# Value products of both halves joined in one group, folds moved to VectorE, first weights behind the last norm

## The chip, the cores and the metric

The kernel runs on one core of one Trainium2 chip. The metric is the device time of one execution, in microseconds (us). The engines are TensorE (PE, matrix products into PSUM), VectorE (DVE), ScalarE (ACT), GpSimd (POOL) and SyncE (SP, which issues transfers). They run side by side, each works off its own queue in order, and they wait for one another through semaphores.

## What is computed

The reference has two parts. The first is chunked attention over 4 batches, 8 heads, 768 positions and 64 columns; each chunk of 32 positions sees its own keys, 16 to the left, 8 to the right and 8 memory keys:

```python
for c in range(nc):
    k_full = np.concatenate([mem_k, k_ctx], axis=2)
    v_full = np.concatenate([mem_v, v_ctx], axis=2)
    scores = scale * np.matmul(q_c, k_full.transpose(0, 1, 3, 2))
    a = np.exp(scores - max); a = a / sum(a)
    out[:, :, c_start:c_end] = np.matmul(a, v_full)
```

The second takes the result as x (4 batches of 768 x 512) through a Fourier mix, a norm and a two-layer network:

```python
X = np.fft.fft(np.fft.fft(x, axis=1), axis=2)
u = x + np.real(X)
un = (u - mean(u)) / np.sqrt(var(u) + 1e-06)
out = u + np.maximum(un @ w_ch1, 0.0) @ w_ch2      # 512 -> 2048 -> 512
```

## The kernel before

**A planner writes the order.** The kernel does not issue its instructions directly. It adds tasks to a `Plan` (lines 37 to 174): an engine, an estimated cost, a function that emits the instructions, the tasks that must be done before, and buffers that are taken and given back (`take`, `give`; with `pick`, whichever of several comes free first). A small event loop then places the tasks, engine by engine, and the instructions are emitted in that order. A task that isn't ready is passed over for a later one of the same engine, so that `ph` and `pc`, which have low rank, fill the holes of attention and Fourier. `behind=` holds a task back until another is placed; `lag=` asks that its inputs have been done for so long already; neither puts a wait into the program. On the chip each engine follows that order strictly.

**Attention** (`attention(n)`, line 869) runs over 16 pairs of heads, four for each batch (HP = 4). For each pair q and k are loaded by POOL's queue (line 347) and v by SP's (line 350), q and k are turned on PE (`trq`, `trk`, line 374) and copied out (`qT`, `kTb`); in batch 3 a transposing transfer does that. Then, for each half g of the positions: scores on PE into `sc` (line 430, 12 matmuls, tile 64*128), two exponentials on ACT (line 438) into one of three `e1` buffers, the value products on PE into `xa` (line 454, 12 fp32 products that the profile shows as 24 matmuls, tile 128*64), and the norm on DVE (lines 464 and 465) into `xsb`. `xa` is one PSUM bank. In batch 0 the second half goes to a bank of `mlp`, named `xo`.

**PSUM** has further banks: `tr` for the turned q and k, `sc`, and two each of `mlp` and `acc`, which `ph`, `pc`, `ps`, `pm`, `tp` share.

**The first Fourier stage** (`first_fourier`, line 983) belongs to batch 0. It folds x in pieces while the pairs of batch 0 finish: `g_zy` (line 594) after two pairs, `g_ff` (lines 608 to 615) once after the third and once after the fourth, then the split into high (ACT, line 629) and low parts (DVE, line 633), and the row transform on PE (`ps`, lines 653 and 666). Until they can begin, PE runs `idle` matmuls (line 830). The first two folds of the half g = 1 are on POOL (`early = ("DVE", "POOL")[g]`); all others are on DVE. Then come `up` (ACT, 538), its rest (DVE, 543), the column transform (`pm`, 677), the sum and the statistics (DVE, 683 and 691), `un` (ACT, 697), and in batch 0 its turn on PE (`tp`, 704) and the copy `unT` (715). The later batches use `fourier(b)` with whole folds on DVE.

**The network** runs over all batches: for each half of the rows 16 blocks `ph` (line 739, four matmuls of 384 columns, then a relu on ACT, line 747), then `pc` (line 754, 16 matmuls of 512 columns for each of three row tiles) and the output sum on DVE (line 779). Its weights w1 and w2 are loaded by POOL's queue (`weights`, lines 975 and 979): w1 behind the k load of pair 5, w2 behind that of pair 6.

Of the kernel before, what the change touches and what calls it, by code (L numbers as in the profile page):

```python
# [177 lines left out]
def kernel(  # L178
# [15 lines left out]
    P = 128  # L194
# [25 lines left out]
    def bank(tag, shape, dtype, name):  # L220
        i = bank_free[tag].pop(0)
        t = fps.tile(shape, dtype, tag=f"{tag}{i}", bufs=1, name=name)
        bank_of[name].append((t, tag, i)) if name in bank_of else bank_of.update({name: [(t, tag, i)]})
        return t
# [125 lines left out]
    def e_load_v(n):  # L350
# [11 lines left out]
        for hh in range(2):  # L362
# [2 lines left out]
            nc.sync.dma_start(v1[MEM0:MEM0 + NMEM, hh, :, 0:D],  # L365
                              mem_v[b, 2 * pr + hh].unsqueeze(1).to_broadcast([NMEM, NT, D]))

    qT_of, kT_of, tr_of, e1_of, sc_of, xa_of, xs = ({} for _ in range(7))

    def turn(out_, src, eye):  # L370
# [70 lines left out]

    def e_values(n, g):
        e1 = e1_of.pop((n, g))
        if n < HP and g == 1:
            xa = bank("mlp", [P, 3, 2, 66], FP32, "xo")
        else:
            xa = aps.tile([P, 3, 2, 66], FP32, tag="xa", bufs=1, name="xa")
        xa_of[n, g] = xa
        for st in range(3):
            for hh in range(2):  # L450
                v1 = va[n % NV]
                for half in range(2):
                    t6 = 2 * st + half
                    nc.tensor.matmul(xa[64 * half:64 * half + 64, st, hh, 0:65],  # L454
                                     e1[:, hh, t6, :], v1[:, hh, 6 * g + t6, 0:65],
                                     start=True, stop=True)

    def e_norm(n, g):
        b, pr = seq[n]
        if b not in xs:  # L460
            xs[b] = apool.tile([P, NST, DM], FP32, tag="xsb", bufs=3, name=f"xsb{b}")
        xa = xa_of.pop((n, g))
        zs = apool.tile([P, 3, 2], FP32, tag="zs", bufs=3, name="zs")
        nc.vector.reciprocal(zs, xa[:, :, :, 64])  # L464
        nc.vector.tensor_tensor(  # L465
            xs[b][:, 3 * g:3 * g + 3, 2 * pr * D:(2 * pr + 2) * D]
            .rearrange("p s (h d) -> p s h d", h=2),
            xa[:, :, :, 0:D], zs.unsqueeze(3).to_broadcast([P, 3, 2, D]), ALU.mult)
        if n < HP and g == 1:
            let_go(xa)  # L470


# [117 lines left out]
    def g_zy(par, g):  # L590
        if g == 0:
            zy_of[0, par] = fpool.tile([P, NST, P], FP32, tag="unT", bufs=2, name="zy0")
        xb, sl, eng = xs[0], slice(3 * g, 3 * g + 3), nc.gpsimd if g == 1 else nc.vector
        eng.tensor_tensor(zy_of[0, par][:, sl], xb[:, sl, 0:P], xb[:, sl, HD:HD + P],
                                ALU.add if par == 0 else ALU.subtract)

    def g_ff(par, ab, g, last):
        if (ab, g, last) == (0, 0, 0):
            ff_of[0, par] = fpool.tile([P, 2, NST, P], FP32, tag="fold", bufs=2, name="ff0")
        xb, sl = xs[0][:, 3 * g:3 * g + 3], slice(3 * g, 3 * g + 3)  # L600
        zy, ff = zy_of[0, par][:, sl], ff_of[0, par][:, ab, sl]
        eng = nc.gpsimd if g == 1 and not last else nc.vector
        plus = ab == par
        if last:
            plus = plus == (par == 0)
        if not last:
            if ab == 0:
                eng.tensor_copy(ff[:, :, 0], zy[:, :, 0])
            elif par == 0:
                eng.memset(ff[:, :, 0:1], 0.0)  # L610
        elif (par, ab) == (1, 1):
            eng.tensor_tensor(ff[:, :, 0], xb[:, :, P], xb[:, :, HD + P], ALU.subtract)
        eng.tensor_tensor(ff[:, :, 1:P], (ff if last else zy)[:, :, 1:P],  # L613
                                rev_ap(xb, 2 * P - 1 + HD * last, P - 1, [[DM, 3]]),
                                ALU.add if plus else ALU.subtract)

# [10 lines left out]
    def g_hi(par, ab, g):  # L627
        sl = slice(3 * g, 3 * g + 3)
        nc.scalar.copy(g_hl(par, 0)[:, ab, sl], ff_of[0, par][:, ab, sl])
# [95 lines left out]

    def slot(b, i):
        return SLOT[i] if b else i

    pick_of = {}

    def pick(*key):
        return pick_of.setdefault(key, dict(of=("mlp", "acc")))
# [136 lines left out]
    def attention(n):  # L869
# [19 lines left out]
        if b >= TURNED:  # L889
            eq = add("SP", 1.2, lambda: e_flip_q(n), [lq], take=("qT",), give=("qs",),  # L890
                     late=5.0, loose=True, behind=t_flip[0])
            t_flip[0] = tk = add("SP", 1.2, lambda: e_flip_k(n), [lk, t_uz], take=("kU",),
                                 give=("ks",), late=5.0, loose=True, behind=eq)
            ek = add("DVE", 0.6, lambda: e_kT(n), [tk, mk], give=("kU",))
        else:
            tq = add("PE", 0.40, lambda: e_turn_q(n), [lq, t_idb], take=("tr",), give=("qs",))
            dve = ("DVE", nc.vector.tensor_copy) if n < HP else ("ACT", None)
            eq = add("ACT", 0.80, lambda: e_qT(n), [tq], take=("qT",), give=("tr",),
                     rank=SINES - 0.5 if n == 0 else None)
            ktag = "acc" if first else "tr"  # L900
            tk = add("PE", 0.43, lambda: e_turn_k(n), [lk, t_idb, t_kz if n == 0 else t_kzs],
                     take=(ktag,), give=("ks",))
            ek = add(dve[0], 1.25 if dve[1] else 1.04, lambda: e_kT(n, dve[1]), [tk, mk],
                     give=(ktag,))
        for g in range(2):
            s_ = add("PE", 0.32, lambda g=g: e_scores(n, g), [eq, ek], take=("sc",),
                     give=("qT", "kTb") if g == 1 else ())
            t_sc[n, g] = s_
            t_exp[n, g] = x_ = add("ACT", 1.12, lambda g=g: e_exp(n, g),
                     [s_, t_masks, t_after.get(n)], take=("e1",), give=("sc",))  # L910
            tag = "mlp" if first and g == 1 else "xa"
            v_ = add("PE", 0.85, lambda g=g: e_values(n, g), [x_, lv, t_low[n % NV]], take=(tag,),
                     rank=len(plan.tasks) + (50 if (n, g) == (2, 1) else 25) if first else None,
                     give=("e1", "va") if g == 1 else ("e1",))
            take = ("xsb",) if g == 0 and n % HP == 0 else ()
            t_norm[n, g] = add("DVE", 0.78, lambda g=g: e_norm(n, g),
                               [v_, t_norm[n - n % HP, 0] if (n % HP, g) != (0, 0) else None],
                               take=take,
                               give=(tag,))
# [48 lines left out]


    w2v = moe_w_ch2.rearrange("(ht p) m -> p ht m", p=P)  # L970
    t_w1, t_w2 = [], []

    def weights(n):
        if n == HP + 1:
            t_w1.extend(add("POOL", 0.7, lambda dt=dt: nc.gpsimd.dma_start(
                w1_sb[:, dt, :], moe_w_ch1[ts(dt, P), :]), moved=2.4, grain=0.32, late=2.0,
                behind=t_ck[n], rank=t_ck[n]["rank"] + 0.1) for dt in range(NDT))
        else:
            t_w2.extend(add("POOL", 0.7, lambda g=g: nc.gpsimd.dma_start(
                w2_sb[:, ts(g, 4), :], w2v[:, ts(g, 4), :]), moved=2.6, late=2.0,  # L980
                behind=t_ck[n], rank=t_ck[n]["rank"] + 0.1) for g in range(4))

    def first_fourier():
        t_rest, t_mid, t_row, pre = {}, {}, {}, {}
        for g in range(2):
            for par in range(2):
                early = ("DVE", "POOL")[g]
                zy = add(early, (0.5, 1.1)[g], lambda par=par, g=g: g_zy(par, g),
                         [t_norm[0, g], t_norm[1, g], t_sines],
                         take=("unT",) if g == 0 else (), rank=20.1 if g else None)  # L990
                for ab in range(2):
                    pre[par, ab, g] = add(early, (0.62 if ab == 0 else 0.5) + 0.8 * g,
                                          lambda par=par, ab=ab, g=g: g_ff(par, ab, g, 0),
                                          [zy, t_norm[2, g]], rank=20.2 + 0.1 * par if g else None,
                                          take=("fold",) if (ab, g) == (0, 0) else (),
                                          give=("unT",) if (ab, g) == (1, 1) else ())
            t_mid[g] = add("POOL", 0.9, lambda g=g: g_mid(g), [t_norm[2, g], t_norm[3, g]],
# [3 lines left out]
            for par in range(2):  # L1001
                for ab in range(2):
                    end = (ab, g) == (1, 1)
                    ff = add("DVE", 0.5 + 0.1 * par * ab,
                             lambda par=par, ab=ab, g=g: g_ff(par, ab, g, 1),
                             [pre[par, ab, g], t_norm[3, g]])
                    hi = add("ACT", 0.5, lambda par=par, ab=ab, g=g: g_hi(par, ab, g), [ff],
                             take=(("hl",), ("hT",))[par] if (ab, g) == (0, 0) else ())
                    lo = add("DVE", 0.48, lambda par=par, ab=ab, g=g: g_lo(par, ab, g), [hi],
# [206 lines left out]
```

The softmax here doesn't subtract the row's maximum and nothing guards it: scores larger than these inputs give would overflow.

## Time and profile before

The median of three runs is 289.14 us (289.12 to 289.34); the profiled span is 287.7 us.

| from the profile | |
|---|---|
| ACT relu, line 747 | 128 times 491 ns, 62.0 us |
| PE `ph`, line 739 | 512 matmuls, 88.5 us busy |
| PE `pc`, line 754 | 368 recorded of 384, 84.2 us busy |
| PE `xa`, line 454 | 672 matmuls, 26.4 us busy |
| DVE busy from 20 to 50 us | 28.4 of 30 us |
| POOL busy from 20 to 50 us | 18.6 of 30 us |
| start of the first `ps` | 33.3 us |
| start of the first `ph` | 57.9 us |
| start of the first `pc` | 72.9 us |
| last `pm` matmuls | 208.0 to 208.8 us |
| unbroken `ph` and `pc` to the end | 208.8 to 284.3 us |

"Busy" is the sum of the durations on an engine. Matmuls overlap one another and their ends are modelled, so what a group of matmuls costs is better read from the distance between the start of its first and the start of what comes next. "Idle before" is time in which an engine had nothing running, put down to what ended it. A row of the timeline gives start, duration, engine, line, operation, output and inputs, the tile in rows*columns for PE, the shapes, and xcount for several merged into one row.

### The profile page before, as it was taken

How to read it: one execution, taken by the hardware profiler on the slowest of the kernel's cores; microseconds unless marked ns; L12 is line 12 of the kernel's file. 1: busy time of each engine (PE TensorE's matmuls, PEld its weight loads, DVE VectorE, ACT ScalarE, POOL GpSimd, SP SyncE). 2: the span in 40 equal slices, each digit the busy share in tenths (PEclk: the TensorE clock that was granted, in tenths of full speed). 3: DMA queues.
4: the chain of work that ended last, by engine and by line, in shares of the span. 5: the costliest groups of instructions: out<-in, count | busy, mean ns of one | idle time of the engine just before them, and what ended most of it. 6: DMA issues, size and time to landing. Idle time of an engine off the chain costs nothing.

```text
span 287.7 us, 7165 instructions
## 1 busy us (share of the span) xinstructions
PE 272.2 (95%) x2947; PEld 172.2 (60%) x2947; DVE 169.5 (59%) x350; ACT 159.9 (56%) x286; POOL 65.7 (23%) x115
## 2 busy tenths in 40 slices
PE   0599889999999999999999999999999999999995
PEld 0476578865565777556766556566654644645644
DVE  7968999862159967958874984985672012012012
ACT  6887345788766676835764485517660721722710
POOL 8844794341210182261001020010020000000000
PEclk9999999999999999999999999999999999999999
DMA  6999999999998999999993756766142504003204
GB/s 108 198 184 162 180 154 204 203 201 196 207 189 219 171 199 153 164 112 238 173 209 86 166 113 108 175 107 195 21 85 84 106 0 117 32 34 100 51 36 109
DMA packets 116112, 39.92 MB, mean 139 GB/s; under 512 B 104560, under 2 KB 111472, under 8 KB 116080
## 3 DMA queue, kind: packets, MB, share of 16 engines
q1 hardware_dynamic: 93888, 23.54, 46.4%
q0 software_dynamic: 21472, 15.21, 32.9%
q10 hardware_dynamic: 720, 0.72, 0.8%
q8 instruction: 23, 0.38, 0.6%
q14 instruction: 9, 0.07, 0.1%
HBM read 37.36 MB, written 13.37 MB: 176 GB/s over the span
## 4 chain that ended last, share of the span: by engine, by line
PE 83%; DMA 6%; DVE 5%; POOL 4%; issue 1%; POOLq 0%
PE pc L754 28%; PE ph L739 26%; PE xa L454 7%; DMA qs<-in_q_dram 6%; PE ps L526 5%; PE pm L677 4%; PE sc L430 3%; DVE ff L613 2%; PE ps L666 2%; PE trk L374 2%; PE trq L374 1%; PE pc L760 1%; PE idle L830 1%; DVE hl L633 1%; DVE xsb L465 1%
## 5 line engine op out<-in xcount | busy, mean ns | idle before, releaser
L747 ACT ACTIVATE hT<-ph 128x384 f16<-128x384 f32 x128 | 62.0, 491 | 50.8 <-PE ph L739 49.9
L739 PE MATMUL ph<-unT,w_sb 128*128 128x384 f16 x512 | 88.5, 326 | 0.0
L754 PE MATMUL pc<-w_sb,hT 128*128 128x512 f16 x368 | 84.2, 380 | 0.0
L739 PEld LDWEIGHTS <-w_sb 128*128 128x128 f16 x512 | 48.4, 98 | 31.7 <-issue 0.6
L754 PEld LDWEIGHTS <-hT 128*128 128x128 f16 x368 | 34.5, 98 | 39.1 <-issue 0.2
L779 DVE SCALAR_TENSOR_TENSOR osb<-pc,rstd,xsb 128x512 f32<-128x512 f32 x23 | 17.2, 750 | 63.8 <-PE pc L754 61.6
L438 ACT ACTIVATE e<-sc,mbias 128x384 f32<-128x384 f32 x64 | 33.6, 577 | 22.7 <-PE sc L430 22.6
L454 PEld LDWEIGHTS xa<-va,e 128*64 128x64 f32 x672 | 22.5, 141 | 7.0 <-issue 5.6
L454 PE MATMUL xa<-va,e 128*64 128x65 f32 x672 | 26.4, 229 | 0.0
L697 ACT ACTIVATE un<-xsb,mu_s 128x512 f16<-128x512 f32 x24 | 17.2, 719 | 7.7 <-DVE mu_s L692 7.7
L538 ACT CAST up<-ps 128x386 f16<-128x386 f32 x16 | 9.6, 602 | 19.6 <-PE ps L526 17.4
L691 DVE BATCH_NORM_STATS2 st<-xsb 128x6 f32<-128x512 f32 x24 | 16.6, 692 | 0.8
L465 DVE TENSOR_TENSOR xsb<-xa,zs 128x384 f32<-128x384 f32 x28 | 15.6, 558 | 1.0
L464 DVE RECIPROCAL zs<-xa 128x6 f32<-128x6 f32 x28 | 5.3, 189 | 17.6 <-PE xa L454 17.6
L543 DVE TENSOR_TENSOR up<-ps,up 128x386 f16<-128x386 f32 x16 | 9.6, 598 | 9.2 <-ACT up L538 9.1
L683 DVE TENSOR_TENSOR xsb<-pm,xsb 128x512 f32<-128x512 f32 x15 | 10.0, 673 | 5.0 <-PE pm L677 5.0
L569 POOL DMA_DIRECT2D xr<-x_back x3 | 2.3, 780 | 46.6 <-DMA x_back<-x_rows 46.6
L430 PEld LDWEIGHTS <-kTb 64*128 64x128 bf16 x384 | 7.7, 97 | 8.7 <-issue 6.8
L430 PE MATMUL sc<-qT,kTb 64*128 64x64 bf16 x384 | 11.6, 196 | 0.9 <-POOL va L315 0.9
L516 DVE TENSOR_TENSOR lo<-ff,hi 128x768 f16<-128x768 f32 x12 | 11.4, 954 | 1.5 <-ACT hi L511 1.3
L486 DVE TENSOR_TENSOR zy<-xsb 128x768 f32<-128x768 f32 x12 | 11.4, 955 | 0.2
L503 DVE TENSOR_TENSOR ff<-pq 128x762 f32<-128x762 f32 x12 | 11.3, 947 | 0.0
(153 smaller groups left out, 355.1 us busy)
## 6 DMA issues: line engine op xcount, KB each, us to landing
va<-in_v_dram SPq DMA_DIRECT2D x32, 220.0 KB
w_sb<-in_moe_w_ch_dram POOLq DMA_DIRECT2D x8, 512.0 KB, 14.7
out_dram<-osb SPq DMA_DIRECT2D x12, 256.0 KB
qs<-in_q_dram POOLq DMA_DIRECT2D x12, 192.0 KB, 6.8
ks<-in_k_dram POOLq DMA_DIRECT2D x12, 192.0 KB, 6.7
x_rows<-xsb POOLq DMA_DIRECT2D x3, 768.0 KB, 5.5
xr<-x_back POOLq DMA_DIRECT2D x3, 768.0 KB, 5.4
out_rows<-osb SPq DMA_DIRECT2D x9, 256.0 KB
```

The costliest lines, as they stand in the source:

```text
L430: nc.tensor.matmul(sc[:, hh, t6, :], kT[r0:r0 + 64, t, :], qT[r0:r0 + 64, ts(t, 64)], start=True, stop=True, tile_position=(r0, 0))
L438: nc.scalar.activation(e1[:, :, :, ts(half, 32)], sc[:, :, 0:6, ts(half, 32)], AFT.Exp, bias=mbias[:, half:half + 1], scale=1.0 / math.sqr ...
L454: nc.tensor.matmul(xa[64 * half:64 * half + 64, st, hh, 0:65], e1[:, hh, t6, :], v1[:, hh, 6 * g + t6, 0:65], start=True, stop=True)
L465: nc.vector.tensor_tensor(xs[b][:, 3 * g:3 * g + 3, 2 * pr * D:(2 * pr + 2) * D] .rearrange("p s (h d) -> p s h d", h=2), xa[:, :, :, 0:D] ...
L526: nc.tensor.matmul(out_[:, sp, :], part[:, ab, sp * 3 + st, c0:c1], tab[:, sp, st, :], start=(st == 0 and i == 0), stop=(st == 2 and i == 1))
L677: nc.tensor.matmul(pm[:, par, :], lhs, rhs[:, par, :], start=(im == 0), stop=(im == 3))
L691: nc.vector.bn_stats(st6, xs[b][:, kt, :])
L697: nc.scalar.activation(un, xs[b][:, kt, :], AFT.Identity, bias=mu_of[b][:, kt, 0:1], scale=-1.0)
L739: nc.tensor.matmul(ph[:, 0:384], w1_sb[:, dt, ts(ht, P)], unT_of[b][:, dt, sh * 384:(sh + 1) * 384], start=(dt == 0), stop=(dt == NDT - 1))
L747: nc.scalar.activation(hT_of[b, sh][:, ht, :], ph[:, 0:384], AFT.Relu, bias=0.0, scale=-1.0)
L754: nc.tensor.matmul(pc_of[b, sh, stl], hT_of[b, sh][:, ht, ts(stl, P)], w2_sb[:, ht, :], start=(ht == 0), stop=(ht == NHT - 1))
L779: nc.vector.scalar_tensor_tensor(osb, pc, rstd_of[b][:, st:st + 1], xs[b][:, st, :], ALU.mult, ALU.add)
```

## The change

It has four parts.

1. In batches 1 to 3 the value products of both halves become one task: PE runs the 12 products of g = 0 and the 12 of g = 1 in a row, after both exponentials. The second half gets a bank of its own, picked from `mlp` and `acc` (before, it took `xa` again after the first norm). The aim is fewer switches on PE, and no wait of the second half for the first norm.
2. In the first Fourier stage the folds of g = 1 that POOL did are done by DVE, in the order that the planner finds.
3. The four w1 loads are held back only until the last norm of batch 0 is placed, and the later q and k loads stand behind them.
4. In batch 3 the copy of the turned k is placed 4 us later than its input allows (`lag=4.0`), to leave the transposing transfers room.

`t_mark` is a list that is filled and not read.

```diff
     def e_values(n, g):
         e1 = e1_of.pop((n, g))
-        if n < HP and g == 1:
-            xa = bank("mlp", [P, 3, 2, 66], FP32, "xo")
+        if g == 1:
+            xa = bank("mlp" if n < HP else pick_of["v", n]["tag"], [P, 3, 2, 66], FP32, "xo")
         else:
             xa = aps.tile([P, 3, 2, 66], FP32, tag="xa", bufs=1, name="xa")
...
-        if n < HP and g == 1:
+        if g == 1:
             let_go(xa)
...
     def g_zy(par, g):
-        xb, sl, eng = xs[0], slice(3 * g, 3 * g + 3), nc.gpsimd if g == 1 else nc.vector
-        eng.tensor_tensor(zy_of[0, par][:, sl], xb[:, sl, 0:P], xb[:, sl, HD:HD + P],
+        xb, sl = xs[0], slice(3 * g, 3 * g + 3)
+        nc.vector.tensor_tensor(zy_of[0, par][:, sl], xb[:, sl, 0:P], xb[:, sl, HD:HD + P],
...
     def g_ff(par, ab, g, last):
-        eng = nc.gpsimd if g == 1 and not last else nc.vector
...
-            ek = add("DVE", 0.6, lambda: e_kT(n), [tk, mk], give=("kU",))
+            ek = add("DVE", 0.6, lambda: e_kT(n), [tk, mk], give=("kU",), lag=4.0)
...
+        xs_ = []
         for g in range(2):
...
+            xs_.append(x_)
+            if not first and g == 0:
+                continue
             tag = "mlp" if first and g == 1 else "xa"
+            if not first:
+                vp = dict(of=("mlp", "acc"))
+                pick_of["v", n] = vp
+                v_ = add("PE", 1.5, lambda: [e_values(n, i) for i in range(2)],
+                         xs_ + [lv, t_low[n % NV]], take=("xa",), pick=vp, give=("e1", "e1", "va"))
+                for i in range(2):
+                    t_norm[n, i] = add("DVE", 0.78, lambda i=i: e_norm(n, i),
+                                       [v_, t_norm[n - n % HP, 0] if (n % HP, i) != (0, 0) else None],
+                                       take=("xsb",) if i == 0 and n % HP == 0 else (),
+                                       give=(("xa",), (vp,))[i])
+                continue
...
     def weights(n):
-                behind=t_ck[n], rank=t_ck[n]["rank"] + 0.1) for dt in range(NDT))
+                behind=t_norm[HP - 1, 1], rank=t_ck[n]["rank"] + 0.1) for dt in range(NDT))
+            t_ck[n] = t_w1[-1]
...
     def first_fourier():
-                early = ("DVE", "POOL")[g]
-                zy = add(early, (0.5, 1.1)[g], lambda par=par, g=g: g_zy(par, g),
+                zy = add("DVE", 0.5, lambda par=par, g=g: g_zy(par, g),
                          [t_norm[0, g], t_norm[1, g], t_sines],
-                         take=("unT",) if g == 0 else (), rank=20.1 if g else None)
+                         take=("unT",) if g == 0 else ())
...
-                    pre[par, ab, g] = add(early, (0.62 if ab == 0 else 0.5) + 0.8 * g,
+                    pre[par, ab, g] = add("DVE", (0.62 if ab == 0 else 0.5),
...
+                    if (par, ab, g) == (0, 0, 1):
+                        t_mark.append(ff)
```

More of the change, by code (lines that the diff above doesn't have):

```diff
@@ L366, in e_load_v @@
                               mem_v[b, 2 * pr + hh].unsqueeze(1).to_broadcast([NMEM, NT, D]))
+    pick_of = {}
     qT_of, kT_of, tr_of, e1_of, sc_of, xa_of, xs = ({} for _ in range(7))
@@ L607, in g_ff @@
             if ab == 0:
-                eng.tensor_copy(ff[:, :, 0], zy[:, :, 0])
+                nc.vector.tensor_copy(ff[:, :, 0], zy[:, :, 0])
             elif par == 0:
-                eng.memset(ff[:, :, 0:1], 0.0)
+                nc.vector.memset(ff[:, :, 0:1], 0.0)
         elif (par, ab) == (1, 1):
-            eng.tensor_tensor(ff[:, :, 0], xb[:, :, P], xb[:, :, HD + P], ALU.subtract)
-        eng.tensor_tensor(ff[:, :, 1:P], (ff if last else zy)[:, :, 1:P],
+            nc.vector.tensor_tensor(ff[:, :, 0], xb[:, :, P], xb[:, :, HD + P], ALU.subtract)
+        nc.vector.tensor_tensor(ff[:, :, 1:P], (ff if last else zy)[:, :, 1:P],
                                 rev_ap(xb, 2 * P - 1 + HD * last, P - 1, [[DM, 3]]),
@@ L727, in slot @@
         return SLOT[i] if b else i
-    pick_of = {}
     def pick(*key):
@@ L970 @@
     w2v = moe_w_ch2.rearrange("(ht p) m -> p ht m", p=P)
-    t_w1, t_w2 = [], []
+    t_w1, t_w2, t_mark = [], [], []
     def weights(n):
@@ L986, in first_fourier @@
             for par in range(2):
-                early = ("DVE", "POOL")[g]
-                zy = add(early, (0.5, 1.1)[g], lambda par=par, g=g: g_zy(par, g),
+                zy = add("DVE", 0.5, lambda par=par, g=g: g_zy(par, g),
                          [t_norm[0, g], t_norm[1, g], t_sines],
-                         take=("unT",) if g == 0 else (), rank=20.1 if g else None)
+                         take=("unT",) if g == 0 else ())
                 for ab in range(2):
-                    pre[par, ab, g] = add(early, (0.62 if ab == 0 else 0.5) + 0.8 * g,
+                    pre[par, ab, g] = add("DVE", (0.62 if ab == 0 else 0.5),
                                           lambda par=par, ab=ab, g=g: g_ff(par, ab, g, 0),
-                                          [zy, t_norm[2, g]], rank=20.2 + 0.1 * par if g else None,
+                                          [zy, t_norm[2, g]],
                                           take=("fold",) if (ab, g) == (0, 0) else (),
```

## The prediction

> **What bounds the kernel now.** I read the busy shares first, then the slices, the waits of TensorE (PE), the chain of waits, and last the timeline of single stretches.
>
> ```profile
> PE 272.2 (95%) x2947; PEld 172.2 (60%) x2947; DVE 169.5 (59%) x350; ACT 159.9 (56%) x286; POOL 65.7 (23%) x115
> ...
> PE   0599889999999999999999999999999999999995
> ...
> PEclk9999999999999999999999999999999999999999
> ```
>
> The reader sees PE busy 95% and full from slice 12 on, at a full clock. PE's listed waits come to about 12 us, 7.2 of them before it begins; none is after 40 us. From 47 us on (the transposes of line 374 after the last `ps`) PE is one unbroken queue, so time is gained in two ways only: fewer PE microseconds after 47 us, or a PE that gets there sooner. The tail of the chain gives clean unit prices:
>
> ```profile
> 211.60 10.36 PE pc L754 x48
> 221.96 10.40 PE ph L739 x64
> ```
>
> One `pc` matmul is 10.36/48 = 0.216 us, eight are 1.73; one `ph` 0.1625. In the middle of the kernel there is something on top. In the timeline the distance from one start to the next shows it:
>
> ```profile
> 85.39 1.90 PE L754 MATMUL pc<-w_sb,hT 128*128 128x512 f16 x8
> 87.22 0.92 PE L454 MATMUL xa<-va,e 128*64 128x65 f32 x24
> 88.07 0.35 PE L430 MATMUL sc<-qT,kTb 64*128 64x64 bf16 x12
> ...
> 30.61 0.92 PE L454 MATMUL xo<-va,e 128*64 128x65 f32 x24
> 31.36 0.51 PE L374 MATMUL trq<-ident_b,qs 96*64 96x96 bf16 x16
> ```
>
> Eight `pc` before a value group take 87.22 - 85.39 = 1.83, where 1.73 is due. A value group takes 0.85 before scores and 0.75 before a transpose. The columns rows*columns name the reason: 128*128, 128*64 and 64*128 are three shapes of the array, and **each change of shape costs 0.10 us**; value groups and transposes share one shape and pay nothing between them.
>
> In the first Fourier stage (25 to 47 us) PE isn't the bound. VectorE (DVE) is:
>
> ```profile
> 26.65 2.34 POOL L594 TENSOR_TENSOR zy<-xsb 128x384 f32<-128x384 f32 x2
> 27.59 1.81 DVE L613 TENSOR_TENSOR ff<-zy,xsb 128x381 f32<-128x381 f32 x2
> 30.08 2.95 DVE L613 TENSOR_TENSOR ff<-zy,xsb 128x381 f32<-128x381 f32 x2
> 33.77 1.02 DVE L613 TENSOR_TENSOR ff<-ff,xsb 128x381 f32<-128x381 f32 x2
> 37.44 2.58 POOL L613 TENSOR_TENSOR ff<-zy,xsb 128x381 f32<-128x381 f32 x2
> 37.81 2.61 DVE L633 TENSOR_TENSOR hl<-ff,hl 128x384 f16<-128x384 f32 x2
> 42.76 1.01 DVE L633 TENSOR_TENSOR hl<-ff,hl 128x384 f16<-128x384 f32 x2
> ```
>
> The same pair of folds is 1.02 us alone and 1.81 or 2.95 beside a GpSimd fold; the pair of low parts 1.01 alone and 2.61 beside one.
>
> **What the Trainium skill says.** "Perfetto Trace Analysis", section Identifying the Most-Contended Engine: matmul busy share is no measure of how near TensorE is to its limit. The trace agrees: modelled ends make PE look full, so I price by starts. "TensorEngine Tiling (Array Packing)", Key Properties: "Mode switching requires drain". That fits the 0.10 us. "SBUF — State Buffer", Who interferes with whom: a VectorE instruction with two SBUF inputs contends with a GpSimd instruction that reads SBUF, and the loser blocks. The DVE rows above agree. "DMA: Bandwidth & Descriptors", Issuing engines are not separate DMA queues: all DMA runs on the same 16 engines. So weights that start early compete with the v loads.
>
> **The change part by part.** The order of the built program's instructions (no times in it) shows what each engine gets.
>
> *Joined values.* Work on PE is unchanged: the same 768 value matmuls (`xa` 672 and `xo` 96 now), the same `ph`, `pc`, `ps`, `pm`. I cut PE's order into runs of one shape, from the first `ps` on: 106 changes before, 87 after. Between 128*128 and 128*64 there are 29+29 before and 19+20 after. Nineteen fewer at 0.10 us: **-2.0 us** (1.9 to 2.0). All of it is on the path, since PE never rests there. For changes around `sc` I have no run without one, so they stand at the same 0.10; they nearly cancel in the count (48 before, 48 after).
>
> What the join adds: the group waits for the second exponential, and on PE everything behind it waits as well. The order puts scores of the second half well ahead (mostly with 0.7 to 4 us of `ph` or `pc` between), and one pair of exponentials is 1.05 us: nothing in most of the 12 groups, 0.3 us in a few. And a bank of `mlp`/`acc` is now held until the second norm on DVE. A `ph` run has its relu start 0.86 us after its first matmul (62.09 to 62.95) and end at 1.35; with four or three banks that hides, with two, a pair of blocks takes about 1.41 instead of 1.30. In DVE's order the second norm of batch 2's first pair stands behind about 9 us of folds; the others follow the first norm more closely. With three banks left the cost is nothing; if every hold left two for some seven blocks it were 12 x 7 x 0.055 = 4.6 us, and half of that where `pc` (one bank for 16 matmuls) fills. I take **+0.4 us**, ends 0 and 2.3.
>
> *Folds on VectorE.* Added to DVE: two `zy` (1.03 the pair at 22.43), two column copies of 0.20, a memset of 0.06 and four folds at 0.5: 3.5 us. Taken away: contention, 1.81-1.02, 2.95-1.02, 2.61-1.01 and a copy of 0.76 that is 0.20 elsewhere: 0.8+1.9+1.6+0.6 = 4.9 us. DVE is 1.4 us lighter. Walking DVE's new order with these durations from the end of the kT copy at 25.6: norms of the last pair end at 32.8 (35.5 before), the first low part of the second half is ready at about 41.1, and PE's last 48 `ps` start there and not at 42.6: 1.5 us earlier. The transposes of k for pair 4 (0.48) already ran in the gap.
>
> Not all of it stays. Behind `ps` PE's order now has scores, a transpose and the second scores of pair 4 before `pm`. The second scores wait for the first exponentials, and on ACT these stand behind the kT copy (1.04) and the last `up`. With the rows of 45.85 to 47.34 I get scores at 45.3, exponentials to 47.4, `pm` from 47.7 (before: from 47.2, with a rest to 48.3 in it). PE idles some 1.3 us there, though it comes out with 1.0 us more attention work done. Then DVE's sums, statistics and copies (8.8 us up to the third `unT`) put the first `ph` at 57.5 to 58, as now (57.9), again with scores done in advance. Carried over: **-0.7 us** (0 to -1.5).
>
> *First weights behind the last norm.* On POOL the four w1 issues leave at about 32 to 34 us and not at 40.6 to 42.8, since POOL has no folds left. The `ph` that needs them is at 57.9 and shows no DMA wait, so by itself this is worth nothing; w2 and the q and k behind it start some 7 us earlier, which takes away the wait of the transpose at 71.44 (0.4 us at most). It competes with the v loads of pairs 4 to 6; they run from 26.7, are needed from 52 on, and I book nothing.
>
> *Later lag for kT in batch 3, fewer fills.* The lag only moves scores in PE's order; fills drop from 35 to 31, all where PE waits. Nothing, hidden by `ph` and `pc` queued.
>
> Sum: 289.14 - 2.0 + 0.4 - 0.7 = **286.8 us**.
>
> **Rivals.** *Everything carries* (0.15): no bank is missed, the first stage keeps 1.5 to 2 us: 289.14 - 2.0 - 1.7 = 285.4. For it: no PE wait today although the attention groups are as tight. Against it: DVE and ACT lie between `ps` and the first `ph`. *Gain eaten by holds* (0.08): +2 us of waits before `ph`, 289.1. *Slower* (0.17): holds at the upper end, 2.3, plus joined groups that wait 0.1 us each for exponentials (1.2), no carry-over, and 0.8 to 1.8 us of w1 slowing the v loads or of late folds: net +1.3 at 290.4. For it: a single group in order on PE makes every late exponential a stop, and ACT is 76 to 85% busy from 50 to 70 us. Against it: relus and exponentials stay the same in number and the groups stand behind scores with filler between.
>
> **How the numbers follow.** Forecast 0.60 at 286.8. Its spread (bank term 0 to 2.3, carry 0 to -1.5) gives 285.6 to 288.4; with the better rival and the level one the range is 285.2 to 289.6, which leaves out the slower case and a little at the bottom. Faster 0.75 (forecast and first rival), same 0.08, slower 0.17.
>
> **What would show it.** Right: PE's blocks ahead of value groups lose their 0.10, some 48 value matmuls run in 1.60 us, DVE folds near 0.5 us each with no GpSimd fold, norms of pair 3 end near 33, the last `ps` near 45 and first `ph` at 57 to 58, and the final unbroken run of `ph` and `pc` starts about 2 us earlier. Wrong: PE waits named to ACT hT, DVE xsb or e in `ph` and `xo` rows past 60 us, DMA waits at `xa`, or a first `ph` past 58.5.

## The result and the profile after

The changed kernel takes 286.55 us (median of 5 runs), the kernel before 289.34 beside it; the ratio is 0.989 (95% interval 0.987 to 0.992). The profiled spans are 284.4 and 287.7 us. Some runs of either kernel are disturbed and come out a few us longer; the medians below take in all runs, the ratios the undisturbed ones alone.

The page after the change, busy shares and slices:

```profile
PE 268.3 (94%) x2943; PEld 171.3 (60%) x2943; DVE 165.9 (58%) x359; ACT 158.8 (56%) x286; POOL 57.4 (20%) x106
...
PE   0599998999999999999999999999999999999995
```

PE is as full as before from slice 12 on. Nothing in these shares tells why the kernel is faster; POOL's 65.7 us became 57.4, since the folds, some 8 us, left it. The gain is read from landmarks: PE's next work after the last `ps` of the first Fourier stage, the first `ph`, and the last run of 64 `ph`, from which on both kernels do the same. Before, and then after:

```profile
46.75 0.55 PE L374 MATMUL trk<-turn_b,ks 100*64 100x100 bf16 x16
57.92 1.47 PE L739 MATMUL ph<-unT,w_sb 128*128 128x384 f16 x8
263.32 10.56 PE L739 MATMUL ph<-unT,w_sb 128*128 128x384 f16 x64
```

```profile
44.05 0.35 PE L431 MATMUL sc<-qT,kTb 64*128 64x64 bf16 x12
55.86 0.82 PE L737 MATMUL ph<-unT,w_sb 128*128 128x384 f16 x4
259.90 10.56 PE L737 MATMUL ph<-unT,w_sb 128*128 128x384 f16 x64
```

So 2.06 us come before the first `ph`, and 1.36 us between it and the tail.

**The first part, on VectorE.** Rows of the timeline after:

```profile
29.54 0.55 DVE L613 TENSOR_TENSOR ff<-zy,xsb 128x381 f32<-128x381 f32 x1
30.18 0.20 DVE L465 RECIPROCAL zs<-xa 128x6 f32<-128x6 f32 x1
...
35.46 1.02 DVE L613 TENSOR_TENSOR ff<-zy,xsb 128x381 f32<-128x381 f32 x2
36.40 0.55 DVE L633 TENSOR_TENSOR hl<-ff,hl 128x384 f16<-128x384 f32 x1
37.87 1.48 DVE L613 TENSOR_TENSOR ff<-ff,xsb 128x381 f32<-128x381 f32 x3
39.27 1.02 DVE L633 TENSOR_TENSOR lo<-ff,hi 128x384 f16<-128x384 f32 x2
```

No fold is longer than 0.56 us, and a merged row of three takes 1.48: from one start to the next it is 0.47. The low parts of the second half begin at 39.27; before, the same pair was split:

```profile
40.35 0.54 DVE L633 TENSOR_TENSOR lo<-ff,hi 128x384 f16<-128x384 f32 x1
42.29 0.55 DVE L633 TENSOR_TENSOR lo<-ff,hi 128x384 f16<-128x384 f32 x1
```

**The second part, on PE.** A joined group after:

```profile
81.92 1.90 PE L752 MATMUL pc<-w_sb,hT 128*128 128x512 f16 x8
83.75 0.92 PE L455 MATMUL xa<-va,e 128*64 128x65 f32 x24
84.50 0.87 PE L455 MATMUL xo<-va,e 128*64 128x65 f32 x24
85.30 0.35 PE L431 MATMUL sc<-qT,kTb 64*128 64x64 bf16 x12
```

The group takes 85.30 - 83.75 = 1.55 us; two separate ones took 0.85 each. That is 0.15 less, and not 0.10: one change of shape is saved, and the second half, directly behind the first, takes 0.80 with the change at its end where a half alone took 0.85. The eight `pc` ahead of it still pay their 0.10 (1.83), but once for both halves.

Two waits stand in PE's timeline between the first `ph` and the tail, where the kernel before had none in its list:

```profile
65.61 0.53 PE L375 MATMUL trq<-ident_b,qs 96*64 96x96 bf16 x16 [0.15 <-DMA qs<-in_q_dram]
166.27 5.45 PE L737 MATMUL ph<-unT,w_sb 128*128 128x384 f16 x32 [0.58 <-ACT hT L745]
```

Read by starts, they cost 0.2 and 0.8 us. The second is a matter of banks. Of the four of `mlp` and `acc`, two are held by second halves of joined groups and one by a column product, so the next `ph` has to wait for the relu of the one before. One of these second halves was made at 157.92 and gets its norm on VectorE only at 167.23:

```profile
157.92 0.87 PE L455 MATMUL xo<-va,e 128*64 128x65 f32 x24
167.23 0.16 DVE L465 RECIPROCAL zs<-xo 128x6 f32<-128x6 f32 x1
```

**An account.** Between the first `ph` and the last run of 64 `ph` I split PE's time into three: the matmuls at the unbroken unit prices of the trace before (`ph` 0.1625, `pc` 0.2159, a value half 0.75, and so on), the changes of array shape in the kernel's own order at 0.10 us each, and the rest. The rest is waits, and a constant 0.6 us or so in `ps` and `pm` blocks. Most of that is changes between 128*128 and the one-column matmuls (128*1), 7 to 10 in a kernel, which this count and the prediction's left out. Where the halves are joined, the rest is also 0.5 us smaller, since 11 second halves take 0.05 us less than the price. The counts of `pc` are complete: what the table ahead of the prediction took for 16 missing records is the last row tile, which runs as 32 matmuls of 256 columns (line 760, 758 after).

| kernel | first `ph` at | matmuls | shape changes | rest | ratio to before (95%) |
|---|---|---|---|---|---|
| before | 57.92 | 195.5 | 90: 9.0 | 0.9 | 1 |
| changed | 55.86 | 195.3 | 72: 7.2 | 1.6 | 0.989 (0.987 to 0.992) |
| E4, no lag | 56.13 | 195.3 | 70: 7.0 | 0.8 | 0.985 (0.983 to 0.986) |
| E5, join alone | 56.86 | 195.5 | 73: 7.3 | 3.4 | 1.002 (1.000 to 1.003) |
| E6, folds alone | 56.80 | 195.1 | 84: 8.4 | 3.4 | 1.006 (1.004 to 1.009) |
| E7, weights alone | 58.23 | 195.5 | 90: 9.0 | 1.3 | 1.000 (0.999 to 1.002) |
| E8, all but the join | 55.54 | 195.1 | 88: 8.8 | 1.9 | 0.995 (0.993 to 0.998) |
| E9, all but the weights | 55.91 | 195.3 | 76: 7.6 | 6.5 | 1.011 (1.006 to 1.017) |
| E10, all but the folds | 57.24 | 195.5 | 72: 7.2 | 2.4 | 0.994 (0.993 to 0.996) |

For the changed kernel: 2.06 us from the first stage, 1.8 from 18 shape changes, 0.2 from work done before the first `ph`, less 0.6 us that the rest grew by: 3.4 us, where the spans differ by 3.3. The 0.6 is net: about 1.0 us of new waits and 0.1 in small pieces, less the 0.5 us of cheaper second halves. Each row is one profiled run, not the median.

### The profile page after: what moved, and what is told of

It is laid out like the page before. It is cut to its first block, busy times and chain, and to the rows that moved or that the text cites. A ratio compares the mean times of both kernels' runs of the same rounds, so it can differ in the third digit from the quotient of the medians.

```text
span 284.4 us, 7145 instructions
## 1 busy us (share of the span) xinstructions
PE 268.3 (94%) x2943; PEld 171.3 (60%) x2943; DVE 165.9 (58%) x359; ACT 158.8 (56%) x286; POOL 57.4 (20%) x106
## 2 busy tenths in 40 slices
DMA packets 116112, 39.92 MB, mean 140 GB/s; under 512 B 104560, under 2 KB 111472, under 8 KB 116080
## 4 chain that ended last, share of the span: by engine, by line
PE 82%; DMA 10%; POOL 5%; issue 1%; DVE 0%; ACT 0%; POOLq 0%; DVEq 0%
PE pc L752 28%; PE ph L737 28%; DMA qs<-in_q_dram 9%; PE ps L527 5%; PE xa L455 4%; PE xo L455 3%; PE ps L666 3%; PE pm L677 3%; PE sc L431 2%; PE idle L828 2%; PE trq L375 1%; PE trk L375 1%; DMA out_dram<-osb 1%; PE pm L578 1%; PE ps L653 1%
## 5 line engine op out<-in xcount | busy, mean ns | idle before, releaser
L455 PEld LDWEIGHTS xa<-va,e 128*64 128x64 f32 x384 | 13.1, 142 | 4.4 <-issue 3.7
L512 ACT CAST hi<-ff 128x768 f16<-128x768 f32 x12 | 9.9, 830 | 9.8 <-DVE ff L504 9.8
L455 PE MATMUL xa<-va,e 128*64 128x65 f32 x384 | 15.3, 231 | 0.0
L455 PE MATMUL xo<-va,e 128*64 128x65 f32 x384 | 14.1, 223 | 0.0
L465 DVE RECIPROCAL zs<-xa 128x6 f32<-128x6 f32 x16 | 3.0, 188 | 17.2 <-PE xa L455 17.2
L455 PEld LDWEIGHTS xo<-va,e 128*64 128x64 f32 x384 | 12.6, 138 | 0.4 <-ACT e L439 0.3
```

## The experiments

### What a change of shape costs

```diff
-                v_ = add("PE", 1.5, lambda: [e_values(n, i) for i in range(2)],
+                v_ = add("PE", 1.5, lambda: [e_values(n, 0), e_between(n), e_values(n, 1)],
...
+    def e_between(n):
+        nc.tensor.matmul(xa_of[n, 0][0:W, 0, 0, 65:66], dz[:, 0:W], dz[:, 0:1],
+                         start=True, stop=True)
```

W is 64 in E1 and 128 in E2. Apart from this matmul, every engine has the order of the changed kernel.

> The changed kernel, with one small matmul more in each of the 12 joined value groups, between the two halves: weights of 128 rows by 64 columns (the shape of the value products), one moving column, into a column of the bank that nothing reads. The order on every engine is otherwise that of the changed kernel. Theory (a change of array shape costs 0.10 us): no shape changes, so 12 x some 0.03 us = 0.3 us more at most than the changed kernel: 286.5 to 286.9 us, 0.990 of the kernel before. Rival (any interruption of a group costs, whatever its shape): about 1 to 2 us more, 287.5 to 288.5.

> The same small matmul, with weights of 128 rows by 128 columns, the shape of ph and pc. Theory: two changes of shape more in each of 12 groups, 12 x 2 x 0.10 = 2.4 us more than with the 128x64 one: 289.0 us or so, level with the kernel before, and in the trace the joined group takes some 1.75 us and not 1.55. Rival (the shape doesn't matter; what the join saved was the wait of the second half for the first norm): within 0.3 us of the 128x64 one.

E1: 288.09 us, ratio 0.995 (0.993 to 0.997). E2: 290.01 us, ratio 1.002 (1.001 to 1.004). The timeline of E1, then of E2:

```profile
83.69 0.92 PE L455 MATMUL xa<-va,e 128*64 128x65 f32 x24
84.44 0.17 PE L460 MATMUL xa<-dz 128*64 128x1 bf16 x1
84.44 0.91 PE L455 MATMUL xo<-va,e 128*64 128x65 f32 x24
85.29 0.35 PE L431 MATMUL sc<-qT,kTb 64*128 64x64 bf16 x12
```

```profile
85.26 0.92 PE L455 MATMUL xa<-va,e 128*64 128x65 f32 x24
86.11 0.18 PE L460 MATMUL xa<-dz 128*128 128x1 bf16 x1
86.22 0.92 PE L455 MATMUL xo<-va,e 128*64 128x65 f32 x24
87.07 0.35 PE L431 MATMUL sc<-qT,kTb 64*128 64x64 bf16 x12
```

With the same shape the group takes 1.60 us, with the other 1.81. The difference, 0.21, is two changes, one at each side of the small matmul: 0.10 to go to 128*128, and with the matmul itself 0.11 until the next half starts. All the groups of both kernels show it but one of E1, which holds a wait. 12 x 0.21 = 2.5 us was due in all; the ratios differ by 0.007, about 2.1 us, and the medians by 1.9. The price of a shape change is shown. What the array does in that time is not.

The two small matmuls also differ in their weights, of 64 and of 128 columns. That isn't the cause. Their weight loads take 112 and 96 ns, so the wider one isn't longer, and in the kernel before a change to matmuls with one column of weights costs the same: 0.18 us from start to start where 0.08 is due.

```profile
98.06 0.24 PE L526 MATMUL ps<-sinS,lo 128*128 128x193 f16 x1
98.24 0.24 PE L526 MATMUL ps<-cosS,hi 128*1 128x193 f16 x1
98.32 0.25 PE L526 MATMUL ps<-cosS,lo 128*1 128x193 f16 x1
```

E1 was slower by some 1.5 us than forecast, and its median lies in the range of the rival. The rival is right in part: 12 x 0.05 = 0.6 us is the interruption, whatever its shape. The small matmul itself takes hardly any time (the second half starts at 84.44 as well), but this half then takes 0.85 to the scores, and not the 0.80 that it takes directly behind the first. In E1's profiled run another 1.3 us is one wait, of the first `ph` of batch 1 for the transposing transfers of `unT`:

```profile
PE ph L741 <- DMA unT<-un: 1.3, 1, 1.3
```

In the trace of the changed kernel SyncE issues these five transfers from 120.15 to 126.63, and the `ph` follows at 128.31 without a wait; in E1 it issues them from 120.26 to 127.73, one of them a microsecond longer, and the `ph` starts at 129.83. From the end of the last issue to the `ph` that is 2.1 us in E1 and 1.7 in the changed kernel, which so seems to have little to spare. Whether the other runs of E1 waited there too isn't known.

### Does a GpSimd instruction hold up VectorE's folds

```diff
+    def g_dup():
+        xb = xs[0][:, 3:6]
+        nc.gpsimd.tensor_tensor(dup, xb[:, :, 0:P], xb[:, :, HD:HD + P], ALU.add)
...
     def g_zy(par, g):
+        if g == 1:
+            g_dup()
...
     def g_ff(par, ab, g, last):
+        if not last and (par == 0 if g == 0 else (par, ab) != (1, 1)):
+            g_dup()
```

> The changed kernel, with seven additions of 128x384 on GpSimd in the first Fourier stage that read xsb and write a scratch tile that nothing reads: four beside the first folds, three beside those of the second half. PE, DVE, ACT and SP have the order of the changed kernel. Theory (GpSimd that reads SBUF blocks VectorE folds): folds beside them take 0.8 to 1 us longer, some 3 to 5 us in all, the last ps ends 2 to 4 us later than 44.05 us and so does the first ph: 288.5 to 290.5 us. Rival (the long folds of the kernel before waited for their inputs, and the shorter list of waits is what helped): DVE folds stay at 0.55 us, the time within 0.5 us of 286.5.

291.27 us, ratio 1.008 (1.005 to 1.012), 4.7 us over the changed kernel. The profiled run is its slowest, 294.70. VectorE and GpSimd in its timeline:

```profile
39.05 3.48 DVE L623 TENSOR_TENSOR ff<-zy,xsb 128x381 f32<-128x381 f32 x2
42.45 1.73 DVE L643 TENSOR_TENSOR hl<-ff,hl 128x384 f16<-128x384 f32 x1
...
39.82 2.29 POOL L595 TENSOR_TENSOR dup<-xsb 128x384 f32<-128x384 f32 x2
42.76 1.00 POOL L595 TENSOR_TENSOR dup<-xsb 128x384 f32<-128x384 f32 x1
```

Two folds that take 1.02 us in the changed kernel take 3.48 beside two additions on GpSimd, and a low part 1.73 in place of 0.55. VectorE's order didn't change, and these rows waited for no input. The mechanism is shown, and the price was underestimated: PE's next work after the last `ps` starts at 52.70 us, 8.65 later than in the changed kernel. Of these, 1.8 were there before the first addition, since this profiled run had stood before a q transfer for 1.36 us at 21 us. VectorE lost 5.4 on its way to the second low parts (46.51 for 39.27, less the 1.8). The last 1.5 are PE's: after stops of 1.9, 0.9 and 0.6 us it ran 20 `ps` at half of its pace, 0.16 us from start to start and not 0.085:

```profile
48.05 0.37 PE L676 MATMUL ps<-odd,lo 128*128 128x193 f16 x1
48.21 0.37 PE L676 MATMUL ps<-odd,hi 128*128 128x193 f16 x1
```

In the first of the rows above VectorE lost 2.46 us beside two additions that took 2.29, which is as good as a full stop. Over all seven it lost 0.8 us for each. The additions read and write, and no run tells which of the two holds VectorE up.

### One part alone

Each of E5 to E7 has one part of the change on the kernel before, in the lines of the diff.

> The kernel before with the joined value groups alone. Shape changes from the first ps on: 88 in PE's order (106 before, 87 with all parts). Theory: -1.8 us of shape changes, nothing in the first Fourier stage, 0 to 0.5 us of new waits: 287.5 to 288.0 us, 0.995 of the kernel before; the first ph stays near 57.9. Rival (all of the gain comes from the first stage, the join only moves waits): 289.3 us, 1.000.

289.46 us, ratio 1.002. The forecast failed, and the time is the rival's. The shape changes fell as counted (73 for 90, 1.7 us), and the first `ph` even came 1.06 us earlier. But the rest grew by 2.5 us. The largest piece in the list of its PE's waits, and the place in its timeline:

```profile
PE pm L678 <- DVE xsb L587: 1.5, 1, 1.5
```

```profile
157.71 2.76 PE L753 MATMUL pc<-w_sb,hT 128*128 128x512 f16 x12
162.01 0.39 PE L678 MATMUL pm<-cosD,up 128*128 128x256 f16 x2 [1.54 <-DVE xsb L587]
```

A column product of batch 2 stands before a bank of `acc` that VectorE's sum has not given back. That sum came late itself, and not for a joined group:

```profile
161.20 0.69 DVE L585 TENSOR_TENSOR xsb<-pm,xr 128x510 f32<-128x510 f32 x1 [2.31 <-DMA xr<-x_back]
```

The planner thought the bank free; the transfer of the mirrored rows was late. Other pieces are 0.8 us before a q transfer and some smaller ones. So the join does what it should to PE's shapes, and in this order other waits take the gain back; that the join as such causes them isn't shown.

> The kernel before with the folds on VectorE alone. Shape changes 99 in PE's order, so -0.7 us. Theory: DVE loses its blocked folds, last ps near 44 us, first ph about 2 us earlier than 57.9: -2 - 0.7, 286.6 us, 0.991; should the planner's order lose some of it again, not above 287.8. Rival (the stage's gain is taken back before the first ph, as the prediction had it for the most part): 288.3 us.

292.38 us, ratio 1.006, and a scatter from 289.5 to 297.2 in twenty runs. Both theories missed. In the profiled run, with 289.87 one of the fastest, the first `ph` came 1.1 us earlier, then the rest took 2.4 us more than before: 1.2 us of a value group before the transfer of the memory values (list of PE's waits), 0.7 us of scores before the copied k, and smaller pieces. What makes most other runs longer still isn't shown.

```profile
PE xa L454 <- DMA va<-in_mem_v_dram: 1.2, 1, 1.2
```

> The kernel before with the first weights behind the last norm alone. Shape changes 106, as before. Theory (w1 is not waited for): within 0.4 us of 289.3. With POOL still doing folds the w1 issues can't leave much earlier. Rival (w1 early relieves the transfers of 50 to 75 us): 0.5 to 1 us faster.

289.41 us, ratio 1.000 (0.999 to 1.002): level, as expected.

### All parts but one

> All parts but the join: folds on VectorE, w1 behind the last norm, the lag. Shape changes 103. Theory: first stage 2 us earlier, -0.3 us of shape changes, the join's -1.6 missing: 287.0 to 287.4 us, 0.993. Rival (the join is most of the gain, since only PE's load after 47 us counts): 288.8 us or more.

287.69 us, ratio 0.995. The first `ph` is at 55.54, so the first stage needs no join. It is 1.7 us behind the changed kernel by the ratios. The shape changes (88 and not 72) are 1.6 us of it. The theory's 0.993 is at the edge of the interval; the rival's 288.8 or more is missed.

> The changed kernel, with the folds of the second half on GpSimd again. Shape changes 87. Theory (join -1.8, first stage lost but for what POOL's order gives, about as with the join alone, plus its waits): first ph at 56.9 to 57.9, 287.5 to 289.0 us. Rival (the join pays only through what it does with the earlier first stage): 289.3 us or slower.

287.70 us, ratio 0.994. First `ph` at 57.24, near the time before, shape changes 72: here the join pays, in company of the w1 part and the lag. It is some 1.5 us behind the changed kernel by the ratios, about the 1.4 by which the first `ph` is later. Its profiled run (288.47) also has a wait of 1.6 us before a q transfer. The theory held.

> The changed kernel, w1 loaded as before (behind the k load of pair 5, the later q and k not behind it). Folds on VectorE alone made a kernel whose time scatters, with a value group that waited 1.2 us for a v transfer; the same folds with the w1 part didn't. Theory (the folds need the w1 part: with POOL free, the transfers are issued in another order, and v is late): 288 us or more, waits of PE on DMA of 1 us or more after 47 us. Rival (w1 is worth nothing in any company; folds alone had an unlucky order): 91 shape changes, so 286.9 us, level with the changed kernel within 0.5.

293.97 us, ratio 1.011. The first `ph` is at 55.91, as in the changed kernel, yet the rest is 6.5 us. Its largest wait, and PE's clock around it in a table of stretches (from:to, length, busy time and count of PE, PEld, DVE, ACT, POOL, then the granted clock, share of DMA and GB/s):

```profile
PE ph L737 <- DMA unT<-un: 2.0, 1, 2.0
```

```profile
130.00:132.00 2.00, 0.75 (x4) 0.13 (x2) 1.54 (x3) 0.93 (x2) 0.85 (x1) 1.00 2.02 105
132.00:134.00 2.00, 1.22 (x4) 0.41 (x4) 1.97 (x3) 0.00 (x0) 0.00 (x0) 0.71 1.31 227
134.00:136.00 2.00, 2.00 (x18) 1.08 (x18) 1.57 (x6) 1.54 (x3) 0.00 (x0) 0.50 1.07 385
136.00:138.00 2.00, 2.00 (x13) 1.03 (x10) 0.75 (x1) 1.43 (x3) 0.00 (x0) 0.93 1.03 274
```

PE stood for 2 us before the transposing transfers of batch 1, and then ran at half clock. The three lower rows lose 0.29, 0.50 and 0.07 of 2 us each, which is 3.4 us at half; by the distance of starts that cost another 1.6. Two waits of `ph` before a relu, at 94 and 97 us, cost 0.7 each, again with two banks held by second halves (made at 84.2 and 91.8, normed by 98.6 and 100.0). This is one run of 291.57 us; the median is 2.4 higher. The theory's time came true, but the waits are not for v, as it had them. The rival (worth nothing in any company) is wrong: without this part the planner writes another order, in which the last three transposes of `unT` of that batch are issued from 125.1 us, where the changed kernel issues five of the six from 120.2 on. Why its order came out so is not settled.

### The lag

> The changed kernel without lag=4.0 on the copy of the turned k in batch 3. Theory (the lag does nothing that can be measured): shape changes are 85 and not 87, so 286.3 us, within 0.5 us of the changed kernel. Rival (the lag keeps PE from standing before scores whose k has not landed): PE waits at sc in batch 3, past 100 us, of 1 to 3 us, 287.5 to 289.5.

> The changed kernel without the lag of 4 us, once more, beside the changed kernel on the same chip. Theory (the lag costs some 0.8 us of waits behind the joined groups): 0.984 to 0.986 of the kernel before, 1 to 1.4 us faster than the changed kernel. Rival (the first measurement was of a kind chip): level with the changed kernel within 0.3 us.

> The changed kernel itself, beside the two others and the one without the lag on the same chip. Theory and rival: 0.989 of the kernel before, as measured; it is the yardstick for the three beside it.

E4: 285.12 us, ratio 0.985. Beside the changed kernel on one chip (E11: 286.75 us, 0.990 with 0.986 to 0.993) it was 286.47 us, 0.989 (0.985 to 0.993). E4 was 1.2 us under its forecast, and the theory of E12 was built on that; the rival of E12 came true. So the lag is worth nothing that can be measured, and the better figure of E4 did not repeat. The kernel without the lag beats the kernel before and is level with the changed one.

## Why the prediction was right, and where it wasn't

It said 286.8 us for 286.55 and a range that holds it. Its terms, one by one:

- *Shape changes, -2.0 us*: right. Counted from the order and priced from the distance of starts, 1.8 us after the first `ph`; E1 and E2 show the price. There is a fourth shape, one column, which the prediction didn't count; it is the same in both kernels.
- *New waits, +0.4*: net 0.6. The hold was foreseen. The long one that the prediction names, of batch 2's first pair, lasted 12 us (84.50 to the end of its norm at 96.5) and cost nothing. But six of the twelve second halves hold their bank for 5 us or more, and where two were held at once it cost 0.8 us (166.27). A wait on a relu was a sign of being wrong; this one is of a size that the range holds. The 0.2 before a q transfer was not foreseen. Against them stand 0.5 us that it didn't have: it expected 1.60 for a joined group, and that is 1.55. In E9 waits of the same name, with two banks held again, cost 1.5 us, so the upper part of the range was not out of reach. In E5 the late bank waited for a transfer and not for a joined group.
- *First stage, -0.7*: mis-sized, 2.06 us. The step that failed is the walk along VectorE's order. I added durations, 0.5 to 0.55 a fold; the next instruction starts after 0.47. The 37 instructions from 25.71 to the first of the second low parts last 16.0 us added up, and run in 14.1. The walk made that part ready at 41.1; it was ready at 39.8, and PE took it up at 39.92. The rest followed: the first scores behind `ps` at 44.05 and not 45.3, the second at 45.7 and not 47.4, `pm` at 46.0 and not 47.7, the stop of PE between them 0.9 us and not 1.3. The order of steps was right: the stage keeps less than the 2.7 us by which `ps` ends earlier. E8 and E10 show that the folds make this gain: the first `ph` is at 55.54 without the join and at 57.24 without the folds.
- *Contention on VectorE*: right in kind (E3). It booked 4.9 us taken away against 3.5 added, and VectorE is the bound of that stage.
- *First weights, nothing*: right alone (E7), wrong in company: without it the planner's order is 2.2% slower (E9 to the changed kernel). The prediction priced what a part does by itself; it had no term for the order that the planner makes of it. That early weights slow the v loads shows in none of these runs.
- *Lag, nothing*: right (E11, E12).

The errors of size leave the prediction 1.1 us short of the 3.4 us between the landmarks. That it is only 0.3 us from the median is luck in part: 0.989 of 289.34 is 286.2, and the profiled run took 286.11. The rival "everything carries" was nearer to the first stage and wrong on the new waits. Two of the prediction's sums don't come out: from 289.14 - 2.0, ends of 0 to 2.3 and 0 to -1.5 give 285.6 to 289.4 and not to 288.4, and the terms of *Slower* add up to +2.3 to +3.3 and not +1.3.

The parts don't add. Alone they are +0.2, +0.6 and 0.0%; together -1.1%. What differs is mostly the rest in the account, 0.8 to 6.5 us: other waits in every order that the planner writes. That its costs meet the chip better in one order than in another is the likely reason; no run tests it.

## What to carry to other kernels

Where TensorE is the bound and its stream mixes array shapes, count the changes of shape in the instruction order and price one from the distance of starts in the trace; grouping what has one shape is worth that number. Where a scheduler writes the order from estimated costs, a part of a change can't be judged alone: try it in company too, and read the waits of each order. Walk along an engine's order with the distance from start to start, not with durations (here 0.47 and 0.55 us a fold, over 1 us in 37 instructions).

## What the runs showed of the hardware

After PE had stood for 2.0 us (E9) its granted clock was half for 3.4 us, which cost 1.6. E3 has two such falls, each again of 3.4 us: one after 1.36 us before a q transfer (0.76, 0.50 and 0.89 in the stretches of 2 us from 22 us on), one after the stops of 1.9, 0.9 and 0.6 us (0.73, 0.50 and 0.91 from 46 us on). A wait of 1.3 us in E1, one of 1.5 in E5 and one of 1.6 in E10 brought no fall. So a stop on PE can cost nearly twice its length; which stops do, these runs don't tell.
